# A retention layer with routed experts: when the first expert's weights are loaded, who stores the layer's rows, and the order of a few matmuls

## The chip, the core and the metric

The kernel runs on one core of a Trainium2 chip. The metric is the device time of one execution in microseconds: 736.68 us, the median of three runs (736.45 to 738.42). The profile is one further execution, of 732.8 us from the first instruction to the last; all times "at" a point below are counted from that start. The engines are named as in the profile: PE (matmuls) and PEld (its weight loads), DVE (VectorE), ACT (ScalarE), POOL (GpSimd) and SP (the engine that only issues transfers).

## What is computed

A retention layer (attention with a decay and no softmax) is followed by a layer of eight experts. A token takes either the expert with the highest logit or, when its "local gate" is 0.5 or more, the expert of the token before it; so the choice runs along the sequence.

```python
# attention: q, k, v are (8, 8, 576, 64), float32
scores = scale * np.matmul(q, k.transpose(0, 1, 3, 2))
Dmat = np.where(rel >= 0, gamma[:, None, None] ** rel[None, :, :], 0.0)
x = np.matmul(scores * Dmat[None], v)          # then (B, H, S, D) -> (B, S, H*D) = (8, 576, 512)
# experts: w1 (8, 512, 1024), w2 (8, 1024, 512)
logits = np.einsum('bsd,de->bse', x, w_gate)
local_gate = 1.0 / (1.0 + np.exp(-np.einsum('bsd,de->bse', x, w_local).squeeze(-1)))
for b in range(B):
    for s in range(S):
        fresh_e = int(np.argmax(logits[b, s]))
        e = fresh_e if s == 0 or local_gate[b, s] < 0.5 else prev_e
        prev_e = e
        out[b, s] = softmax(logits[b, s])[e] * (np.maximum(x[b, s] @ w1[e], 0.0) @ w2[e])
```

There are 4608 tokens of 512 features.

## The kernel before

**Attention (lines 145 to 252).** The tokens are cut into 36 chunks of 128. Nine chunks (two sequences of 576) make a period; `m` is a chunk's place in it. For a chunk, `scores` has SP load 1 MB (`ld`: q and k by feature, k and v by token) into one of seven buffers, DVE multiplies q by the decay (`qT`, line 165), POOL multiplies v by it (`vs`, line 169, four buffers), PE forms the scores of the chunk with itself (`sps`, line 176), and DVE masks them (`sT`, line 180). `outputs` multiplies them by `vs` (`ops`, line 201), adds the product of the queries with the state of all earlier chunks of the sequence (line 210), and ACT copies the result to `xT` (line 213). `state` adds the chunk's keys and values to that state (`kv`, line 227; ACT copies it, line 230). `rows` forms the gate products of the chunk (`gps`, line 238: four matmuls, one per 128 features, into four separate strips of 32 partitions; ACT copies them to `parts`, line 241), and turns the rows for storing (line 247, DVE). After every second chunk ACT issues four stores (line 250) of 128 KB each to `xd` in memory, 256 pieces of 512 bytes each. `logits` sums the four strips with one more matmul (`lps`, line 260).

The order on PE is written by hand: at step `i` come the scores of chunk `i + 1`, the outputs of chunk `i`, the state of chunk `i + 1`, the rows of chunk `i - 1`, the logits of chunk `i - 2`, then one step of each running routing. On the other engines a scheduler sets the order by what is ready. All transfers issued by SP and ACT share eight completion slots in turn, so an issue waits until the transfer eight before it has landed, whoever issued that one.

**Routing (lines 267 to 374 and 492 to 627).** Logits are collected in groups of chunks (`GROUPS`, 8, 8, 6, 7 and 7 of them) and ACT copies a group to `lt` (line 265). Then `route` finds each token's expert and its place among that expert's tokens, in a chain of some 45 small operations that goes from DVE to PE and back three times. When the last group is done, DVE and POOL build `values` (line 549), PE sums them (`places`, line 108) into the list of slots, and DVE derives which block takes which tokens (`desc`).

**Experts (lines 633 to 811).** Tokens are worked on in blocks of one expert, up to 768 tokens each. Two blocks' weights (`w1s`, `w2s`) are in fast memory at a time. POOL gathers a block's rows from `xd` (line 640) and loads the next weights (line 674). In `block`, PE first finishes group 0 of the block before (`first_group`), then runs the first layer (line 745; eight passes `m`, each of four matmuls for every piece of at most 512 tokens; ACT applies the ReLU into `hT`, line 747), then the second layer for a narrow remainder (line 710) and for groups 1 and up of 128 tokens each (line 683; ACT scales the result into `ys`, line 687). POOL scatters `ys` to the output (line 662) in order: group 0 of the block before, groups 1 to 5, two narrow pieces, all behind the whole block (lines 797 to 799).

Two things fill the time of the last routing. An **early block** (`block(-1, TSOON)`, line 766) runs 256 tokens of expert 0 that were routed from the first three groups. Its weights, those of expert 0, are what lines 158 to 163 load: 16 pieces of 256 KB, w1 and w2 in turn, behind the loads of chunks 4, 6, ... 34. And in block 0 the rows are turned by PE (`turn`, line 727) between the matmuls of the early block's last group, instead of by DVE.

Of the kernel before, what the change touches and what calls it, by code (L numbers as in the profile page):

```python
# [12 lines left out]
F32 = mybir.dt.float32  # L13
# [19 lines left out]
HALF = S - P * MID  # L33
assert HALF == P // 2 and NTOK % (2 * S) == 0

GROUPS = (8, 8, 6, 7, 7)
Q = max(GROUPS)
assert sum(GROUPS) == NCH

SOON, TSOON = 3, 2 * P  # L40
FULL = 512
# [21 lines left out]
def kernel(  # L63
# [55 lines left out]
    with ExitStack() as part:  # L119
# [25 lines left out]
        def scores(i):  # L145
            m = i % PER
            g = chunks[i]
            ld = raw.tile([P, 4, D], F32, name="ld")
            if i == MID:
                nc.sync.dma_start(out=decq[:, m].rearrange("p c t -> p (c t)"), in_=dq[:, 1])  # L150
            elif 0 < i < PER:
                for c in range(HP):
                    nc.scalar.activation(decq[:, m, c], decq[:, 0, c], Act.Copy, scale=later_q[:, m, c:c + 1])
            cut = 4 if i == 0 else 1
            for k in range(0, 4, 4 // cut):
                loaded = nc.sync.dma_start(out=ld[:, k:k + 4 // cut].rearrange("p t x -> p (t x)"),
                                           in_=qkv[i][:, k * D:(k + 4 // cut) * D])
            if 4 <= i < 4 + 4 * FK and i % 2 == 0:

                k, t = divmod(i // 2 - 2, 2)  # L160
                with tc.issue_after(loaded.ins):
                    nc.sync.dma_start(out=(w2s[0][:, k] if t else w1s[0][:, k].rearrange("p k f -> p (k f)")),
                                      in_=(w2 if t else w1)[0][:, k * D:(k + 1) * D])
# [5 lines left out]
            scaled = nc.gpsimd.tensor_tensor(  # L169
                vs.rearrange("p (h d) -> p h d", h=H), vn.rearrange("p (h d) -> p h d", h=H),  # L170
                deck[:, m, :].unsqueeze(2).to_broadcast([P, H, DH]), op=Alu.mult)
# [12 lines left out]

            with tc.issue_after(scaled.ins):
                for write in to_lanes[:2]:
                    write()
            del to_lanes[:2]

        def outputs(i):  # L190
            m = i % PER
            g = chunks[i]
            qT, vs, sT = g["qT"], g["vs"], g["sT"]


            ops = ps_o.tile([P, 2, HP, P], F32, name="ops")
            for c in range(HP):
                for u in range(2):
                    r = slice((u ^ c & 1) * DH, ((u ^ c & 1) + 1) * DH)
                    h = 2 * c + u  # L200
                    nc.tensor.matmul(ops[r, c & 1, c // 2, :], lhsT=vs[:, h * DH:(h + 1) * DH], rhs=sT[:, u, c, :],  # L201
                                     start=(c < 2), stop=(m == 0), skip_group_check=True)
# [9 lines left out]
            g["xT"] = xT = work.tile([P, HP, P], F32, name="xT", bufs=2)  # L212
            nc.scalar.copy(xT.rearrange("p (a b) t -> p b a t", b=2), ops[:, :, 0:HP // 2])  # L213

        def state(i):
# [14 lines left out]
                nc.scalar.copy(states[i % 2], kv)  # L230

        def rows(i):
            nonlocal x
            xT = chunks[i]["xT"]
# [5 lines left out]
            parts = work.tile([P, P], F32, name="parts")  # L240
            nc.scalar.copy(parts, gps)
            chunks[i]["parts"] = parts


            if i % 2 == 0:
                x = work.tile([P, 2, NSQ, DK, SQ], F32, name="x", bufs=2)
            nc.vector.transpose(x[:, i % 2], xT.rearrange("p c (t s) -> p t c s", s=SQ))  # L247
            if i % 2:
                for a in range(NSQ):
                    nc.scalar.dma_start(  # L250
                        out=xd[(i - 1) * P:(i + 1) * P, a * P:(a + 1) * P].rearrange("(t s) d -> s t d", s=SQ),
                        in_=x[a * SQ:(a + 1) * SQ].rearrange("p b t c r -> p (b t) (c r)"))

        def logits(i):

            nonlocal lt, lps
            i0 = max(k for k in starts if k <= i)
            if i == i0:
                lps = ps_g.tile([P, Q, GW], F32, name="lps")
            nc.tensor.matmul(lps[:, i - i0, :], lhsT=chunks[i]["parts"], rhs=add_parts, start=True, stop=True,  # L260
                             skip_group_check=True)
            if i in ends:
                n = i + 1 - i0
                lt = rt.tile([P, Q, GW], F32, name="lt")
                nc.scalar.copy(lt[:, 0:n], lps[:, 0:n])

# [181 lines left out]
        lt = lps = x = None  # L448

        add_parts = once.tile([P, GW], F32, name="add_parts")  # L450
        for c in range(DK):
            nc.gpsimd.tensor_copy(add_parts[c * SQ:(c + 1) * SQ], ident[c * SQ:(c + 1) * SQ, c * SQ:c * SQ + GW])
# [262 lines left out]
    def block(j, T):  # L715
# [4 lines left out]
        xT = xTs[j % 2]  # L720

        def turn(g, M):
            xps = next(hps_).rearrange("p (c t) -> p c t", c=DK)
# [33 lines left out]
        for g, M in groups[1:]:  # L757
            if M == P:
                group(j, g)

# [10 lines left out]
        weights(j + 1, False)  # L771
        load_tokens(j + 1)

    def store_rest(j):
        for g in range(1, GMAX):
            store(ys[:, g], rows_of[j % 2][:, g:g + 1])
        for M in NARROW:
            store(narrow_ys[M], narrow_rows[j % 2][M], P // M)
# [94 lines left out]
```

## Time and profile before

| stage of the profile | from, to (us) | what happens |
|---|---|---|
| attention | 0 to 170.8 | 36 chunks; `xT` of the first at 12.27, of the last at 168.71 |
| last routing, early block | 170.8 to 207 | PE begins the early block's first layer at 179.69, `places` at 194.75 |
| block 0 begins | 207 to 227.4 | group 0 of the early block and the turning of rows; first layer of block 0 at 227.44 |
| experts | 227.4 to 716.1 | PE busy throughout |
| end | 716.1 to 732.8 | last results copied and scattered; the program's end |

| engine | busy us | share of the span |
|---|---|---|
| PE | 688.8 | 94% |
| PEld | 455.2 | 62% |
| POOL | 232.9 | 32% |
| DVE | 182.1 | 25% |
| ACT | 145.0 | 20% |

The shares are averages over stages that differ: DVE, at 25% overall, is busy four fifths of the time in attention and nearly idle later. How to read the rows that follow: a group of instructions is written as line, engine, operation, what it writes and reads, shape and count, then busy time and the mean of one in ns, then how long the engine had been idle ahead of these instructions and what ended that idleness. A float32 matmul appears as two records, so 36 of them read x72. In the row of 40 slices, each digit is the busy share of a slice of 18.3 us in tenths, and PEclk is the clock granted to PE in tenths of full speed.

Transfers: 54.80 MB on SP's queue, 9.82 MB on ACT's and 50.36 MB on POOL's. The median load of a chunk lands 8.2 us after its issue, the median store of x rows after 5.3 us.

### The profile page before, as it was taken

How to read it: one execution, taken by the hardware profiler on the slowest of the kernel's cores; microseconds unless marked ns; L12 is line 12 of the kernel's file. 1: busy time of each engine (PE TensorE's matmuls, PEld its weight loads, DVE VectorE, ACT ScalarE, POOL GpSimd, SP SyncE). 2: the span in 40 equal slices, each digit the busy share in tenths (PEclk: the TensorE clock that was granted, in tenths of full speed). 3: DMA queues.
4: the chain of work that ended last, by engine and by line, in shares of the span. 5: the costliest groups of instructions: out<-in, count | busy, mean ns of one | idle time of the engine just before them, and what ended most of it. 6: DMA issues, size and time to landing. Idle time of an engine off the chain costs nothing. (4 is left out here: it accounts for less than half of the span.)

```text
span 732.8 us, 12623 instructions
## 1 busy us (share of the span) xinstructions
PE 688.8 (94%) x4960; PEld 455.2 (62%) x4960; DVE 182.1 (25%) x488; ACT 145.0 (20%) x375; POOL 232.9 (32%) x337
## 2 busy tenths in 40 slices
PE   5997999997989999999999999999999999999990
PEld 4876877785734547646754764675487467548640
DVE  5757769887900100200020010002001000200200
ACT  6221222223111112111211110221021112112100
POOL 5232525525270036008102700720270081035013
PEclk9998999997998999999999999999999999999996
DMA  8999999832085018405711740571175067014311
GB/s 336 335 345 356 382 348 339 302 96 51 2 254 116 1 47 303 94 3 206 229 24 62 298 107 3 178 242 33 57 284 128 7 229 199 4 62 140 74 36 49
DMA packets 72013, 116.55 MB, mean 159 GB/s; under 512 B 9160, under 2 KB 52300, under 8 KB 67408
## 3 DMA queue, kind: packets, MB, share of 16 engines
q1 hardware_dynamic: 34688, 54.80, 23.9%
q0 software_dynamic: 17184, 50.36, 18.8%
q10 hardware_dynamic: 20016, 9.82, 4.8%
q8 instruction: 66, 1.08, 0.7%
q14 instruction: 59, 0.48, 0.2%
HBM read 90.82 MB, written 24.12 MB: 157 GB/s over the span
## 5 line engine op out<-in xcount | busy, mean ns | idle before, releaser
L745 PE MATMUL hps<-xT,w1s 128*128 128x304 f32 (+4 forms) x1024 | 258.4, 414 | 0.7 <-ACT xT L729 0.7
L745 PEld LDWEIGHTS hps<-xT,w1s 128*128 128x128 f32 x1024 | 195.6, 191 | 65.0 <-issue 14.0
L683 PE MATMUL yps<-w2s,hT 128*128 128x512 f32 x528 | 232.5, 599 | 1.1 <-issue 1.1
L683 PEld LDWEIGHTS yps<-w2s,hT 128*128 128x128 f32 x528 | 100.0, 191 | 125.2 <-issue 124.9
L662 POOL DMA_INDIRECT out_dram<-ys,rows x49 | 48.8, 996 | 342.1 <-ACT ys L687 329.8
L747 ACT ACTIVATE hT<-hps 128x304 f32<-128x304 f32 (+4 forms) x128 | 53.1, 418 | 202.7 <-PE hps L745 193.7
L655 DVE STREAM_TRANSPOSE xT<-squares 128x512 f32<-128x512 f32 x48 | 29.4, 677 | 198.9 <-PE yps L710 150.7
L644 DVE CAST both<-slot 128x6 f32<-128x6 int32 x9 | 1.6, 172 | 259.0 <-POOL slot L638 259.0
L169 POOL TENSOR_TENSOR vs<-ld,decs 128x512 f32<-128x512 f32 x36 | 39.0, 1086 | 81.2 <-PE ops L201 42.1
L176 PE MATMUL sps<-qT,ld 64*128 64x128 f32 x576 | 49.1, 303 | 14.0 <-DMA ld<-in_qkv_dram 6.8
L640 POOL DMA_INDIRECT xg<-xd,slot x54 | 55.1, 1020 | 19.8 <-issue 13.0
L176 PEld LDWEIGHTS sps<-qT,ld 64*128 64x128 f32 x576 | 40.6, 202 | 17.4 <-DVE sT L180 8.6
L687 ACT ACTIVATE ys<-yps,slot 128x512 f32<-128x512 f32 x31 | 21.3, 688 | 147.3 <-PE yps L683 146.7
L180 DVE TENSOR_TENSOR sT<-sps,mask 128x512 f32<-128x512 f32 x72 | 45.8, 676 | 11.0 <-PE sps L176 10.3
L201 PE MATMUL ops<-sT,vs 128*64 128x128 f32 x576 | 42.4, 291 | 1.8 <-ACT xT L213 0.9
L213 ACT COPY xT<-ops 128x512 f32<-128x512 f32 x36 | 21.1, 587 | 111.4 <-PE ops L210 74.5
L201 PEld LDWEIGHTS ops<-sT,vs 128*64 128x64 f32 x576 | 33.1, 143 | 6.8 <-POOL vs L169 1.2
L165 DVE TENSOR_TENSOR qT<-ld,decq 128x512 f32<-128x512 f32 x36 | 31.4, 876 | 6.9 <-DMA ld<-in_qkv_dram 3.5
L247 DVE STREAM_TRANSPOSE x<-xT 128x512 f32<-128x512 f32 x36 | 25.3, 703 | 22.8 <-DMA xd<-x 18.3
L710 PE MATMUL yps<-w2s,hT 128*32 128x128 f32 (+1 forms) x544 | 30.1, 306 | 0.0
L710 PEld LDWEIGHTS yps<-w2s,hT 128*32 128x32 f32 (+1 forms) x544 | 21.2, 118 | 5.2
L227 PE MATMUL kv<-vs,ld 128*64 128x64 f32 (+1 forms) x512 | 22.5, 232 | 0.6 <-POOL one_of_blk L418 0.6
(194 smaller groups left out, 360.3 us busy)
## 6 DMA issues: line engine op xcount, KB each, us to landing
ld<-in_qkv_dram SPq DMA_DIRECT2D x35, 1024.0 KB, 8.2
w1s<-in_w_dram POOLq DMA_DIRECT2D x32, 512.0 KB
w2s<-in_w_dram POOLq DMA_DIRECT2D x32, 512.0 KB
squares<-xg SPq DMA_DIRECT2D x128, 96.0 KB, 2.3
xd<-x ACTq DMA_DIRECT2D x72, 128.0 KB, 5.3
w1s<-in_w_dram SPq DMA_DIRECT2D x8, 256.0 KB, 7.2
w2s<-in_w_dram SPq DMA_DIRECT2D x8, 256.0 KB, 6.7
ld<-in_qkv_dram SPq DMA_DIRECT2D x4, 256.0 KB, 5.8
```

What stands on the lines that cost most here:

```text
L165: nc.vector.tensor_tensor(qT, ld[:, 0].rearrange("p (c s) -> p c s", c=HP), decq[:, m], op=Alu.mult)
L169: scaled = nc.gpsimd.tensor_tensor(vs.rearrange("p (h d) -> p h d", h=H), vn.rearrange("p (h d) -> p h d", h=H), deck[:, m, :].unsqueeze(2 ...
L176: nc.tensor.matmul(sps[u][:, c, :], lhsT=kT[r, c, :], rhs=qT[r, c, :], start=True, stop=True, skip_group_check=True)
L180: nc.vector.tensor_tensor(sT[:, u], sps[u], (mask2 if m == MID else mask).unsqueeze(1).to_broadcast([P, HP, P]), op=Alu.mult)
L201: nc.tensor.matmul(ops[r, c & 1, c // 2, :], lhsT=vs[:, h * DH:(h + 1) * DH], rhs=sT[:, u, c, :], start=(c < 2), stop=(m == 0), skip_group ...
L640: nc.gpsimd.indirect_dma_start(out=xgs[j % 2][:, g, :], out_offset=None, in_=xd, in_offset=bass.IndirectOffsetOnAxis(ap=slot[:, g, 0:1], a ...
L655: nc.vector.transpose(xTs[j % 2][:, :, g * P:(g + 1) * P].rearrange("p c (t s) -> p t c s", s=SQ), squares[:, g].rearrange("p t (c r) -> p ...
L662: nc.gpsimd.indirect_dma_start(out=next(views).rearrange("t (q d) -> (t q) d", q=n), out_offset=bass.IndirectOffsetOnAxis(ap=rows, axis=0) ...
L683: nc.tensor.matmul(yps, lhsT=hT[:, m, g * P:(g + 1) * P], rhs=w[:, m, :], start=(m == 0), stop=(m == FK - 1))
L710: nc.tensor.matmul(yps[q * M:(q + 1) * M, 0:D // n], lhsT=hT[:, m, first:first + M], rhs=w[:, m, q * D // n:(q + 1) * D // n], start=(m == ...
L745: nc.tensor.matmul(hps[:, 0:T // n], lhsT=w[:, m, c, :], rhs=xT[:, c, cols], start=(c == 0), stop=(c == DK - 1))
L747: nc.scalar.activation(hT[:, m, cols], hps[:, 0:T // n], Act.Relu)
```

## The change

It has five parts.

1. The weights of the first expert no longer come between chunks 4 and 34. The eight pieces of w1 come behind the loads of the last eight chunks, and w2 comes in four pieces of 512 KB behind the last load. This leaves the early loads of q, k and v to themselves.
2. Gates of two chunks at once: `rows` runs on every second step for two chunks. Their products are summed over two of the four feature strips in place, so that both chunks fit into one tile of 128 partitions, and one copy and one logits matmul serve two chunks. The groups become 8, 8, 6, 8 and 6, all even.
3. In `outputs` the product with the past state stands ahead of the product with `sT`, so that PE has work that doesn't need the newest mask.
4. POOL issues the stores of x rows, so that ACT's queue, and the completion slots of the loads, are free of them. `xT` gets three buffers, `parts` two.
5. In the last block that is always run (`j == NSURE - 2`) the second layer of group 1 is taken out of the block and put behind a second branch. The stores of the narrow pieces and of groups 2 to 5 are issued ahead of it. In all blocks the narrow pieces are now stored first.

```diff
-GROUPS = (8, 8, 6, 7, 7)
+GROUPS = (8, 8, 6, 8, 6)
...
-            if 4 <= i < 4 + 4 * FK and i % 2 == 0:
-
-                k, t = divmod(i // 2 - 2, 2)
+            k = i - NCH + FK
+            if k >= 0:
                 with tc.issue_after(loaded.ins):
-                    nc.sync.dma_start(out=(w2s[0][:, k] if t else w1s[0][:, k].rearrange("p k f -> p (k f)")),
-                                      in_=(w2 if t else w1)[0][:, k * D:(k + 1) * D])
+                    nc.sync.dma_start(out=w1s[0][:, k].rearrange("p k f -> p (k f)"),
+                                      in_=w1[0][:, k * D:(k + 1) * D])
+            if i == NCH - 1:
+                for k in range(0, FK, 2):
+                    with tc.issue_after(loaded.ins):
+                        nc.sync.dma_start(out=w2s[0][:, k:k + 2].rearrange("p k f -> p (k f)"),
+                                          in_=w2[0][:, k * D:(k + 2) * D])
...
-            for c in range(HP):
-                for u in range(2):
-                    ...
-                    nc.tensor.matmul(ops[r, c & 1, c // 2, :], lhsT=vs[:, h * DH:(h + 1) * DH], rhs=sT[:, u, c, :],
-                                     start=(c < 2), stop=(m == 0), skip_group_check=True)
             if m > 0:
                 ...
                         nc.tensor.matmul(ops[r, c & 1, c // 2, 0:n], lhsT=states[(i + 1) % 2][k, c, :],
-                                         rhs=qT[k, c, 0:n], start=False, stop=True, skip_group_check=True)
+                                         rhs=qT[k, c, 0:n], start=(c < 2), stop=False, skip_group_check=True)
+            for c in range(HP):
+                for u in range(2):
+                    ...
+                    nc.tensor.matmul(ops[r, c & 1, c // 2, :], lhsT=vs[:, h * DH:(h + 1) * DH], rhs=sT[:, u, c, :],
+                                     start=(m == 0 and c < 2), stop=True, skip_group_check=True)
...
             for c in range(DK):
-                nc.tensor.matmul(gps[c * SQ:(c + 1) * SQ, :], lhsT=gates[:, c, :], rhs=xT[:, c, :],
-                                 start=True, stop=True, skip_group_check=True)
+                for b in range(2):
+                    r = slice((2 * b + c % 2) * SQ, (2 * b + c % 2 + 1) * SQ)
+                    nc.tensor.matmul(gps[r, :], lhsT=gates[:, c, :], rhs=xTs[b][:, c, :],
+                                     start=(c < 2), stop=(c >= 2), skip_group_check=True)
...
-            if i % 2:
-                for a in range(NSQ):
-                    nc.scalar.dma_start(
+            for a in range(NSQ):
+                nc.gpsimd.dma_start(
...
-            nc.tensor.matmul(lps[:, i - i0, :], lhsT=chunks[i]["parts"], rhs=add_parts, start=True, stop=True,
-                             skip_group_check=True)
+            nc.tensor.matmul(lps[:, i - i0:i - i0 + 2, :].rearrange("p c e -> p (c e)"), lhsT=chunks[i]["parts"],
+                             rhs=add_parts, start=True, stop=True, skip_group_check=True)
...
-                if 0 <= i - 1 < NCH:
-                    rows(i - 1)
+                if i % 2 == 0 and 0 <= i - 2:
+                    rows(i - 2)
                 if 0 <= i - 2:
-                    logits(i - 2)
+                    if i % 2:
+                        logits(i - 3)
...
+        apart = j == NSURE - 2
         for k in tc.Switch({ET.PE: kind, ET.Activation: kind}, len(SIZES) + 1):
             ...
             elif SIZES[k] and j < NBLK:
-                block(j, SIZES[k])
+                block(j, SIZES[k], 0 if apart else None)
         store(ys[:, 0], rows_of[j % 2][:, 0:1])
-        if j != NSURE - 1:
+        if apart:
+            store_rest(j, range(2, GMAX))
+            for k in tc.Switch({ET.PE: kind, ET.Activation: kind}, len(SIZES) + 1):
+                if k < len(SIZES) and SIZES[k]:
+                    block(j, SIZES[k], 1)
+            store_rest(j, (1,), ())
+        elif j != NSURE - 1:
             store_rest(j)
```

In the changed program's order, PE runs 7 of the 32 first-layer matmuls of the early block ahead of `places` and 25 behind it; in the program before these are 25 and 7. ACT's copies of the early block's turned rows stand, in the changed order, behind its twelve lane operations of the last group (lines 362 and 363 of the kernel before).

More of the change, by code (lines that the diff above doesn't have):

```diff
@@ L34 @@
 assert HALF == P // 2 and NTOK % (2 * S) == 0
-GROUPS = (8, 8, 6, 7, 7)
+GROUPS = (8, 8, 6, 8, 6)
 Q = max(GROUPS)
-assert sum(GROUPS) == NCH
+assert sum(GROUPS) == NCH and not any(n % 2 for n in GROUPS)
 SOON, TSOON = 3, 2 * P
@@ L196, in outputs @@
             ops = ps_o.tile([P, 2, HP, P], F32, name="ops")
-            for c in range(HP):
-                for u in range(2):
-                    r = slice((u ^ c & 1) * DH, ((u ^ c & 1) + 1) * DH)
-                    h = 2 * c + u
-                    nc.tensor.matmul(ops[r, c & 1, c // 2, :], lhsT=vs[:, h * DH:(h + 1) * DH], rhs=sT[:, u, c, :],
-                                     start=(c < 2), stop=(m == 0), skip_group_check=True)
             if m > 0:
@@ L210, in outputs @@
                         nc.tensor.matmul(ops[r, c & 1, c // 2, 0:n], lhsT=states[(i + 1) % 2][k, c, :],
-                                         rhs=qT[k, c, 0:n], start=False, stop=True, skip_group_check=True)
-            g["xT"] = xT = work.tile([P, HP, P], F32, name="xT", bufs=2)
+                                         rhs=qT[k, c, 0:n], start=(c < 2), stop=False, skip_group_check=True)
+            for c in range(HP):
+                for u in range(2):
+                    r = slice((u ^ c & 1) * DH, ((u ^ c & 1) + 1) * DH)
+                    h = 2 * c + u
+                    nc.tensor.matmul(ops[r, c & 1, c // 2, :], lhsT=vs[:, h * DH:(h + 1) * DH], rhs=sT[:, u, c, :],
+                                     start=(m == 0 and c < 2), stop=True, skip_group_check=True)
+            g["xT"] = xT = work.tile([P, HP, P], F32, name="xT", bufs=3)
             nc.scalar.copy(xT.rearrange("p (a b) t -> p b a t", b=2), ops[:, :, 0:HP // 2])
@@ L232, in rows @@
         def rows(i):
-            nonlocal x
-            xT = chunks[i]["xT"]
+            xTs = [chunks[i + b]["xT"] for b in range(2)]
             gps = ps_g.tile([P, P], F32, name="gps")
             for c in range(DK):
-                nc.tensor.matmul(gps[c * SQ:(c + 1) * SQ, :], lhsT=gates[:, c, :], rhs=xT[:, c, :],
-                                 start=True, stop=True, skip_group_check=True)
-            parts = work.tile([P, P], F32, name="parts")
+                for b in range(2):
+                    r = slice((2 * b + c % 2) * SQ, (2 * b + c % 2 + 1) * SQ)
+                    nc.tensor.matmul(gps[r, :], lhsT=gates[:, c, :], rhs=xTs[b][:, c, :],
+                                     start=(c < 2), stop=(c >= 2), skip_group_check=True)
+            parts = work.tile([P, P], F32, name="parts", bufs=2)
             nc.scalar.copy(parts, gps)
             chunks[i]["parts"] = parts
-            if i % 2 == 0:
-                x = work.tile([P, 2, NSQ, DK, SQ], F32, name="x", bufs=2)
-            nc.vector.transpose(x[:, i % 2], xT.rearrange("p c (t s) -> p t c s", s=SQ))
-            if i % 2:
-                for a in range(NSQ):
-                    nc.scalar.dma_start(
-                        out=xd[(i - 1) * P:(i + 1) * P, a * P:(a + 1) * P].rearrange("(t s) d -> s t d", s=SQ),
-                        in_=x[a * SQ:(a + 1) * SQ].rearrange("p b t c r -> p (b t) (c r)"))
+            x = work.tile([P, 2, NSQ, DK, SQ], F32, name="x", bufs=2)
+            for b in range(2):
+                nc.vector.transpose(x[:, b], xTs[b].rearrange("p c (t s) -> p t c s", s=SQ))
+            for a in range(NSQ):
+                nc.gpsimd.dma_start(
+                    out=xd[i * P:(i + 2) * P, a * P:(a + 1) * P].rearrange("(t s) d -> s t d", s=SQ),
+                    in_=x[a * SQ:(a + 1) * SQ].rearrange("p b t c r -> p (b t) (c r)"))
         def logits(i):
@@ L259, in logits @@
                 lps = ps_g.tile([P, Q, GW], F32, name="lps")
-            nc.tensor.matmul(lps[:, i - i0, :], lhsT=chunks[i]["parts"], rhs=add_parts, start=True, stop=True,
-                             skip_group_check=True)
-            if i in ends:
-                n = i + 1 - i0
+            nc.tensor.matmul(lps[:, i - i0:i - i0 + 2, :].rearrange("p c e -> p (c e)"), lhsT=chunks[i]["parts"],
+                             rhs=add_parts, start=True, stop=True, skip_group_check=True)
+            if i + 1 in ends:
+                n = i + 2 - i0
                 lt = rt.tile([P, Q, GW], F32, name="lt")
@@ L447 @@
         last_e = low[:, 0:1]
-        lt = lps = x = None
-        add_parts = once.tile([P, GW], F32, name="add_parts")
+        lt = lps = None
+        add_parts = once.tile([P, 2 * GW], F32, name="add_parts")
+        nc.gpsimd.memset(add_parts, 0.0)
         for c in range(DK):
-            nc.gpsimd.tensor_copy(add_parts[c * SQ:(c + 1) * SQ], ident[c * SQ:(c + 1) * SQ, c * SQ:c * SQ + GW])
+            r = slice(c * SQ, (c + 1) * SQ)
+            nc.gpsimd.tensor_copy(add_parts[r, c // 2 * GW:(c // 2 + 1) * GW], ident[r, c * SQ:c * SQ + GW])
         for M, at in ((P // 2, 0), (P // 4, 0), (P // 4, P // 2)):
@@ L713, in narrow, with block @@
         nc.scalar.activation(narrow_ys[M], yps[:, 0:D // n], Act.Copy, scale=share)
-    def block(j, T):
+    def block(j, T, part=None):
         xg = xgs[j % 2]
@@ L720, in block @@
         xT = xTs[j % 2]
+        if part == 1:
+            if groups[1:] and groups[1][1] == P:
+                group(j, 1)
+            return
         def turn(g, M):
@@ L756, in block @@
                 first += M
-        for g, M in groups[1:]:
+        for g, M in groups[1 if part is None else 2:]:
             if M == P:
@@ L772, in load_next, with store_rest @@
         load_tokens(j + 1)
-    def store_rest(j):
-        for g in range(1, GMAX):
+    def store_rest(j, groups=range(1, GMAX), sizes=NARROW):
+        for M in sizes:
+            store(narrow_ys[M], narrow_rows[j % 2][M], P // M)
+        for g in groups:
             store(ys[:, g], rows_of[j % 2][:, g:g + 1])
-        for M in NARROW:
-            store(narrow_ys[M], narrow_rows[j % 2][M], P // M)
     def step(j):
```

## Prediction

> **What bounds the kernel now.** I read the slices of the span first, then a table of stretches, then the groups, the waits and two spots of the timeline.
>
> ```profile
> PE   5997999997989999999999999999999999999990
> PEclk9998999997998999999999999999999999999996
> DMA  8999999832085018405711740571175067014311
> ```
>
> From the 13th slice on (220 us) PE is full to the end, so the change can shorten nothing of the expert stage but its last microseconds. What the change can move is the front: attention up to about 171 us, routing up to 227 us, and the tail. A table of stretches cuts the front (engine order: PE, PEld, DVE, ACT, POOL busy us with instruction counts, then clock, DMA share, GB/s):
>
> ```profile
> 24.00:54.00 30.00, 29.94 (x552) 24.43 (x548) 20.95 (x29) 7.61 (x21) 8.80 (x8) 1.00 0.91 323
> 54.00:60.00 6.00, 1.16 (x8) 0.97 (x9) 2.93 (x5) 0.88 (x4) 1.04 (x1) 0.70 1.04 342
> 60.00:96.00 36.00, 36.00 (x644) 29.63 (x642) 29.52 (x73) 8.98 (x25) 15.44 (x24) 0.95 1.02 378
> 96.00:102.00 6.00, 4.49 (x77) 3.46 (x77) 1.97 (x7) 1.81 (x6) 1.35 (x2) 1.00 0.90 298
> 102.00:141.00 39.00, 36.47 (x617) 29.40 (x621) 31.91 (x90) 9.13 (x28) 16.81 (x31) 1.00 1.00 346
> ...
> 192.00:195.00 3.00, 1.71 (x18) 1.52 (x17) 2.86 (x8) 0.21 (x1) 0.00 (x0) 1.00 0.03 8
> 195.00:207.00 12.00, 12.00 (x53) 7.46 (x50) 7.16 (x51) 0.77 (x2) 4.79 (x7) 1.00 0.39 124
> 207.00:227.44 20.44, 15.69 (x146) 7.64 (x146) 0.24 (x2) 3.00 (x7) 11.19 (x13) 0.83 0.64 195
> ```
>
> In attention PE is the bound with holes: from 24 to 141 us it is idle 0.06 + 4.84 + 0 + 1.51 + 2.53 = 8.9 us, 9.5 us to 171. The largest hole (54 to 60) is followed by three microseconds at half clock, 1.5 us more. DMA is full all that time, so the holes are loads that came late. The waits of the DMA issuer (SP) say why:
>
> ```profile
> SPq L156 <- DMA xd<-x: 36.7, 8, 8.9
> SPq L162 <- DMA xd<-x: 34.5, 9, 10.9
> ```
>
> SP stood 71 us behind stores of x: before it may issue a load, it waits for the completion slot that an earlier store of x, issued by ACT, still holds.
>
> Groups that price the edits (busy us, mean ns, idle before):
>
> ```profile
> L260 PE MATMUL lps<-add_parts,parts 128*128 128x10 f32 x72 | 14.0, 268 | 0.1
> L169 POOL TENSOR_TENSOR vs<-ld,decs 128x512 f32<-128x512 f32 x36 | 39.0, 1086 | 81.2 <-PE ops L201 42.1
> L640 POOL DMA_INDIRECT xg<-xd,slot x54 | 55.1, 1020 | 19.8 <-issue 13.0
> L674 POOL DMA_DIRECT2D w2s<-in_w_dram x32 | 15.8, 530 | 0.4 <-issue 0.2 <-DMA w2s<-in_w_dram 0.2
> ```
>
> And three instructions of the timeline: the copy that starts the last routing, the last result, the last store.
>
> ```profile
> 172.04 0.22 ACT L265 COPY lt<-lps 128x70 f32<-128x70 f32 x1 [1.71 <-DMA xd<-x]
> ...
> 716.14 0.69 ACT L687 ACTIVATE ys<-yps,slot 128x512 f32<-128x512 f32 x1 [0.48 <-PE yps L683]
> ...
> 720.63 0.98 POOL L662 DMA_INDIRECT out_dram<-ys,rows  x1 [0.30 <-issue]
> ```
>
> **What the Trainium skill says.** "DMA: Bandwidth & Descriptors", section "Issuing engines are not separate DMA queues": whoever issues, the transfers share the same 16 engines. So moving the x stores to GpSimd buys no bandwidth; the gain can only lie in who waits for whom. The trace agrees (DMA share 0.9 to 1.0 with three issuers). The same page, "SWDGE vs HWDGE vs iDMA": descriptors of a DMA issued by GpSimd are built in software there, so each costs that engine time; the trace has 0.53 to 1.02 us for one, against medians of 0.43 us on ACT's queue and 0.33 us on SP's. "SBUF — State Buffer", section "SBUF: two separate sides": while VectorE runs certain copies GpSimd cannot write descriptors, with 620 ns growing to 3100 in its example. Here the two indirect loads in attention, beside a VectorE busy 80%, took 1.14 us against 1.02 later: I expect little of it. "TensorE: Matmul & The Clock Gate", "What's actually happening": idle PE falls to half clock after about 3.4 us; the hole at 54 us agrees (clock 0.50 from 57 to 63).
>
> **The change part by part.**
>
> *Weights of the first expert* (16 loads of 256 KB in chunks 4 to 34; after: eight with chunks 28 to 35, then four of 512 KB). Same bytes, 4.2 MB; at the 378 GB/s of the stretch from 60 to 96 us 11 us of DMA leave the stretch in which PE starves. The late ones run behind SP's loads, where DMA before was busy 0.40 on average (141 to 171 us). They are needed at about 180 us: free. In the last eight chunks a load comes to 1.31 + 0.26 MB per chunk, 4.2 us; seven buffered chunks cover that.
>
> *x stores to GpSimd.* SP's 71 us behind stores vanish, so loads run up to seven ahead. Together with the weights I let this take 7 of the 11 us (9.5 of holes and 1.5 of half clock); VectorE, busy 29.52 of 36 us, so 3.2 us of a chunk step that shrinks to 3.8, keeps the rest. GpSimd gets 72 issues. Their cost isn't in the trace: each has 256 pieces of 512 B, where the direct weight load has 128 pieces (0.56 back to back) and the gather 128 rows (1.02, with 0.3 between). Bounds 0.56 and 1.3; I take 0.85. Total 61 us on top of 34 vs of 1.08 (37), 15 for lanes, 8 of casts and gathers: 121 of the 136 us from 20 to 156. Not the bound, though near it. Behind a waiting store stands the next vs; it runs about two chunk steps (7.6 us) ahead of its matmul, and four stores are 3.4: hidden.
>
> *Gates of two chunks at once.* The gate matmuls stay 8 per pair; the logits matmuls halve. One costs PE a step of 0.32 us (46.30 less 45.98 between starts in the timeline): 18 x 0.32 = **5.8 us** off the bound engine. The copies of parts (18 x 0.27 us of ACT) lie beside it: nothing.
>
> *Past states first.* The same matmuls in another order; the wait for sT is already short (PE waits 15 us for sT in all, before the scores): nothing counted apart from the holes.
>
> *Routing.* ACT no longer issues four stores before the logits copy: the 1.71 us wait goes, of which a step for the paired logits takes 0.7: -1.0. The last group has 6 chunks, not 7: -0.3. Against it, the order on PE: before, 25 of the 32 first-layer matmuls of the early block stand ahead of the matmuls that place the tokens, and 7 behind; after, 7 ahead and 25 behind. Moved behind: 18 x 0.434 = 7.8 us (each m of 4 took 1.73). ACT's copy into xT now also stands behind 12 lane operations, so PE begins the block some 5 us later. PE's holes ahead (2.6 us at 192) grow and pay nothing. What comes back: from 207 to 227.4 PE took 20.4 us for 7.0 of matmuls and some 4.7 of turns; it waited for gathers and instructions. With the early block later, gathers have landed and the weight loads of block 1 are mostly through; I take 16 us, bounds 12 and 20. Net -1.3 + 7.8 - 4.4 = **+2.1 us** (bounds -2 and +6.5).
>
> *Tail.* Before, eight stores of 1.3 us wait for the whole of block 7 and begin at 710.24; the last comes 5.5 us after PE ends (721.61 less 716.14). After, seven begin one group (6.86 us) earlier, and the last two fit right behind their results: 716.14 + 0.69 + 0.1 + 1.0 = 717.9, -3.7 us. The extra branch may cost up to 1 us: **-3.0**.
>
> Sum: -7 - 5.8 + 2.1 - 3.0 = -13.7; 736.68 - 13.7 = **723.0 us**.
>
> **The rivals.**
> - *All holes close.* -11 and -5.8 in attention, turns in 13 us (-0.9 in routing), tail -3.7: -21.4, 715 us. For it: PE is the one full engine. Against: VectorE at 85%.
> - *The routing eats it.* Holes refilled by vs or sT waits (-2), -5.8, +6.5, -2.5: -3.8, 733 us. For it: the moved 7.8 us stand on PE's path for sure.
> - *Nothing left.* As that one, with a GpSimd just at its limit that holds PE for 4 us: 737 us.
> - *GpSimd becomes the bound*, slower. At 1.3 us a store 94 + 59 = 153 us from 20 on: attention ends at 173, +2; routing +5, tail -3: 741 us. Half a microsecond more a store, if VectorE locks it out: 777. Against: the two gathers at 1.14.
>
> **How the numbers follow.** Forecast 0.58; all holes 0.14; routing eats it 0.11; nothing left 0.04; GpSimd bound 0.13. Faster 0.83, same 0.04, slower 0.13. The range leaves out the last two: from 713 (under the second case) to 735 (above the third).
>
> **What would show it.** Logits matmuls x36 at the same mean. SP without waits on xd. No stretch of attention under 90% PE; the last copy of xT (168.71 before) at 155 to 157. A store on GpSimd at 0.6 to 1.0 us. PE's first block-0 stretch at 215 to 217 instead of 227.4. Last store within 2 us of PE's end. Wrong if a store is over 1.1 us with vs waited for by PE, or if the early block begins later than 20 us behind the last xT.

## Result, and the profile after

The changed kernel takes **725.59 us** (median of 4 runs, 723.37 to 725.80) against 737.24 us (4 runs, 736.45 to 738.42): a ratio of 0.9834, 95% interval 0.9809 to 0.9858. The forecast was 723.0, with 713 to 735 as its range. Where some executions of a program were slow as a whole (two of the twelve of `e1_stores_act`), they count neither in its median nor in its ratio. The profiled executions of the two kernels span 732.8 and 723.8 us. The total came out close to the forecast: 11.7 us less by the medians, 9.0 in this pair of profiles, against 13.7. The parts did not, so they are set side by side first (us, from the timelines of the two profiles):

| step | before | after | difference | predicted |
|---|---|---|---|---|
| start to last copy of `xT` | 168.71 | 151.71 | -17.0 | -12.8 |
| last `xT` to first layer of block 0 | 58.73 | 64.13 | +5.4 | +2.1 |
| block 0 to PE's end | 488.66 | 491.55 | +2.9 | } |
| PE's end to last store's issue | 4.53 | 1.00 | -3.5 | } -3.0 |
| last store's issue to the end | 12.16 | 15.44 | +3.3 | } |
| sum | 732.8 | 723.8 | -9.0 | -13.7 |

The slices of the changed kernel (18.1 us each):

```profile
PE   5999998963999999999999999999999999999980
PEclk9999999995999999999999999999999999999996
DMA  8999999530462038218402830760184075024220
```

Attention ends one slice earlier, in the 9th, and a new hole stands in the 9th and 10th, the 10th at half clock. The table of stretches shows it (engine order PE, PEld, DVE, ACT, POOL, then clock, DMA share, GB/s):

```profile
24.00:60.00 36.00, 34.70 (x669) 29.67 (x669) 28.80 (x55) 10.15 (x26) 25.17 (x31) 1.00 1.02 415
60.00:96.00 36.00, 34.22 (x641) 29.45 (x640) 32.92 (x76) 9.15 (x24) 27.22 (x42) 0.95 0.95 348
96.00:120.00 24.00, 22.11 (x418) 18.70 (x414) 21.38 (x54) 6.20 (x17) 18.56 (x31) 1.00 1.01 389
...
159.00:172.00 13.00, 5.27 (x14) 4.08 (x15) 12.32 (x36) 4.51 (x15) 12.36 (x14) 0.61 0.00 1
172.00:186.00 14.00, 6.96 (x43) 5.99 (x43) 9.01 (x32) 0.38 (x1) 7.38 (x7) 0.63 0.00 1
```

From 24 to 60 us the transfers ran at a share of 1.02 and moved 415 GB/s; before, the stretches of that table with a share of 1.00 or more moved 342 to 378. From 159 to 186 us PE worked 12.2 of 27 us at a clock of about 0.6. The groups that were priced, and what SP now waits for (total, times, longest):

```profile
L266 PE MATMUL lps<-add_parts,parts 128*128 128x20 f32 x36 | 7.3, 279 | 0.4 <-ACT parts L248 0.4
L256 POOL DMA_DIRECT2D xd<-x x72 | 42.6, 597 | 12.0 <-DVE x L254 5.8 <-DVE run L309 1.9 <-DVE fr L298 1.8
L174 POOL TENSOR_TENSOR vs<-ld,decs 128x512 f32<-128x512 f32 x36 | 40.9, 1143 | 16.9 <-DMA ld<-in_qkv_dram 8.4 <-PE ops L215 5.3 <-issue 2.8
...
SPq L156 <- PE kv L232: 88.8, 26, 7.1
```

A store costs GpSimd 0.60 us, not the 0.85 taken. SP no longer waits for stores of x; it waits for buffers that PE has still to release, so loads run as far ahead as the seven buffers allow. Last, PE's way through the routing, before and after, and the last result and the last store after:

```profile
179.69 12.53 PE L745 MATMUL hps<-xT,w1s 128*128 128x256 f32 x50 [0.69 <-ACT xT L729]
193.51 3.58 PE L108 MATMUL places<-w1s,lanes 128*128 128x220 bf16 x36 [1.29 <-DVE first L573]
```

```profile
165.80 5.27 PE L758 MATMUL hps<-xT,w1s 128*128 128x256 f32 x14 [7.45 <-ACT xT L742]
179.04 5.71 PE L108 MATMUL places<-w1s,lanes 128*128 128x220 bf16 x36 [7.97 <-DVE its_n L606]
...
707.43 0.69 ACT L696 ACTIVATE ys<-yps,slot 128x512 f32<-128x512 f32 x1 [1.38 <-PE yps L692]
708.39 0.98 POOL L671 DMA_INDIRECT out_dram<-ys,rows  x1 [5.26 <-ACT ys L696]
```

The brackets are PE's idle time ahead of the early block's first layer and of `places`: 15.4 us together, against 2.0 before. In the profile before, `places` begins at 193.51; the 194.75 of the table of stages was the edge of a window.

### The profile page after: what moved, and what is told of

Same layout as the page of the kernel before. It is cut to its first block, busy times and chain, and to the rows that moved or that the text cites. A ratio compares the mean times of both kernels' runs of the same rounds, so it can differ in the third digit from the quotient of the medians.

```text
span 723.8 us, 12549 instructions
## 1 busy us (share of the span) xinstructions
PE 672.0 (93%) x4924; PEld 447.9 (62%) x4924; DVE 185.9 (26%) x488; ACT 141.6 (20%) x355; POOL 284.2 (39%) x411
## 4 chain that ended last, share of the span: by engine, by line
issue 56%; PE 16%; POOL 12%; DMA 8%; DVE 5%; POOLq 2%; ACT 0%; SPq 0%; DVEq 0%; ACTq 0%
POOL xg L649 5%; PE sps L181 4%; PE ops L215 4%; POOL out_dram L671 3%; DMA out_dram<-ys,rows 3%; DMA w2s<-in_w_dram 3%; PE ops L209 2%; PE kv L232 2%; PE gps L245 1%; DMA xd<-x 1%; POOL w1s L683 1%; PE places L108 1%; DVE sT L185 1%; DMA ld<-in_qkv_dram 1%; POOLq L683 1%
## 5 line engine op out<-in xcount | busy, mean ns | idle before, releaser
L758 PEld LDWEIGHTS hps<-xT,w1s 128*128 128x128 f32 x1024 | 195.8, 191 | 71.3 <-issue 13.7
L649 POOL DMA_INDIRECT xg<-xd,slot x54 | 54.8, 1015 | 21.1 <-issue 12.8
L181 PE MATMUL sps<-qT,ld 64*128 64x128 f32 x576 | 46.9, 295 | 11.2 <-DVE past L324 6.2
L181 PEld LDWEIGHTS sps<-qT,ld 64*128 64x128 f32 x576 | 38.8, 196 | 16.6 <-DVE sT L185 7.1
L174 POOL TENSOR_TENSOR vs<-ld,decs 128x512 f32<-128x512 f32 x36 | 40.9, 1143 | 16.9 <-DMA ld<-in_qkv_dram 8.4
L256 POOL DMA_DIRECT2D xd<-x x72 | 42.6, 597 | 12.0 <-DVE x L254 5.8
```

Source lines behind the costliest of these rows:

```text
L174: scaled = nc.gpsimd.tensor_tensor(vs.rearrange("p (h d) -> p h d", h=H), vn.rearrange("p (h d) -> p h d", h=H), deck[:, m, :].unsqueeze(2 ...
L256: nc.gpsimd.dma_start(out=xd[i * P:(i + 2) * P, a * P:(a + 1) * P].rearrange("(t s) d -> s t d", s=SQ), in_=x[a * SQ:(a + 1) * SQ].rearran ...
L649: nc.gpsimd.indirect_dma_start(out=xgs[j % 2][:, g, :], out_offset=None, in_=xd, in_offset=bass.IndirectOffsetOnAxis(ap=slot[:, g, 0:1], a ...
L758: nc.tensor.matmul(hps[:, 0:T // n], lhsT=w[:, m, c, :], rhs=xT[:, c, cols], start=(c == 0), stop=(c == DK - 1))
```

## The experiments

"Last xT" below is the start of the last copy of `xT`. In two profiles of the changed kernel itself it came at 151.71 and 148.37, so a difference of 3 us in one profile says little.

### Who stores x

`e1_stores_act`, the changed kernel with

```diff
-                nc.gpsimd.dma_start(
+                nc.scalar.dma_start(
```

> The changed kernel with one edit undone: ACT issues the x stores again. Theory (stores held the loads, so GpSimd's issues are worth most of the attention's gain): SP waits for completion slots of stores again (over 30 us), the last copy of xT moves from 151.7 to 156-162, median 727 to 732. Rival (weights and gates alone made the gain): last xT within 1 us of 151.7. On the end of the program: if its final drain on GpSimd, 8.9 us in the changed kernel and 6.0 before, grows with the number of GpSimd's transfers, it is back at 6.0 here; if it has another cause, it stays at 8.9.

```profile
SPq L156 <- DMA xd<-x: 38.5, 9, 7.9
SPq L156 <- DMA ld<-in_qkv_dram: 17.4, 5, 6.9
```

Measured: last xT at **168.43**, median 736.68 us (ten runs), ratio to before 0.9979 (0.9945 to 1.0013). One edit undone takes the whole gain, although weights, gates and order stay changed. SP waits behind slots again, 71 us up to the last xT (the two longest groups are shown). The theory's direction holds, but the effect is stronger than the 4 to 10 us expected of it, and its reason had to be tested. The drain at the end is back at 5.96 us.

`e12_act_long_pieces`: ACT issues, but in long pieces, which leaves the rows of x in other places than the gathers read.

```diff
-                nc.gpsimd.dma_start(
-                    out=xd[i * P:(i + 2) * P, a * P:(a + 1) * P].rearrange("(t s) d -> s t d", s=SQ),
-                    in_=x[a * SQ:(a + 1) * SQ].rearrange("p b t c r -> p (b t) (c r)"))
+                nc.scalar.dma_start(
+                    out=xd[i * P + a * 2 * SQ:i * P + (a + 1) * 2 * SQ].rearrange("(s t) d -> s (t d)", t=2),
+                    in_=x[a * SQ:(a + 1) * SQ].rearrange("p b t c r -> p (b t c r)"))
```

> As e1_stores_act (ACT issues the x stores, which hold completion slots as before), but each store of 128 KB goes out in 32 pieces of 4 KB instead of 256 of 512 bytes. The rows of x land in other places than the gathers expect, so the expert stage works on other rows in the same numbers. Theory (the 512-byte pieces of ACT's stores took the time of the transfers): last xT at 151 to 156 although ACT issues. Rival (it is ACT's queue or the slots, whatever the pieces): last xT at 163 to 169, as in e1 (168.4). The final drain: 6.0 us, since GpSimd issues no store of x.

```profile
SPq L156 <- DMA ld<-in_qkv_dram: 25.9, 7, 7.0
SPq L156 <- DMA xd<-x: 19.7, 8, 5.7
```

Measured: last xT at **147.00**, median 715.07 us, ratio 0.9700 (0.9637 to 0.9763). Same issuer and same slots as in e1, same bytes, 21 us apart: it is the size of the pieces. The transfers from 24 to 126 us (for each queue its packets, MB and share of 16 engines; q1 is SP's queue, q10 ACT's, q0 GpSimd's), first before, then the changed kernel, then e1, then e12:

```profile
DMA packets 17669, 35.42 MB, mean 347 GB/s; under 512 B 1316, under 2 KB 12902, under 8 KB 14477
q1 hardware_dynamic: 5347, 29.22, 76.8%
q10 hardware_dynamic: 12303, 5.93, 20.1%
```

```profile
DMA packets 7838, 39.25 MB, mean 385 GB/s; under 512 B 1426, under 2 KB 1426, under 8 KB 4191
q1 hardware_dynamic: 5329, 32.17, 80.8%
q0 software_dynamic: 2488, 6.79, 17.4%
```

```profile
DMA packets 16228, 32.59 MB, mean 320 GB/s; under 512 B 1161, under 2 KB 12611, under 8 KB 13101
q1 hardware_dynamic: 4053, 26.47, 71.5%
q10 hardware_dynamic: 12157, 5.87, 20.4%
```

```profile
DMA packets 7774, 39.00 MB, mean 382 GB/s; under 512 B 1439, under 2 KB 1439, under 8 KB 4138
q1 hardware_dynamic: 5155, 31.59, 81.0%
q10 hardware_dynamic: 2598, 7.12, 17.7%
```

Over the whole span, by the queue totals of each page less what the same queue carries without them, ACT's 72 stores are 19,584 packets (272 each: the 256 pieces and 16 more); GpSimd's stores of the same 512-byte pieces are 3,456 (48 each: 128 KB in 4 KB packets are 32, and 16 more), exactly as many as ACT's in 4 KB pieces. In the window of 102 us, a stored megabyte takes 20.1% of 102 us / 5.93 = 3.46 us of all 16 engines before and 17.4% of 102 us / 6.79 = 2.61 us after; a loaded one takes 2.68 and 2.56 us. For 9.44 MB of x and 42 MB of loads and weights the difference is 8.0 + 5.0 = 13 us of full transfers. By this estimate packets account for 13 of the 17 us; the rest lies within what gates and the spread between executions leave. The same sum from e1 to e12 (3.54 to 2.54 us for a stored megabyte, 2.76 to 2.62 for a loaded one) gives 9.5 + 5.9 = 15 of the 21 us. In e1 the transfers also stood still: its queues fill 93% of the window, against nearly 100% in e12, which is 7 us. What held them back there was not told apart.

`e10_slots_held` tests the other reason: GpSimd stores, and each store has a companion of 128 bytes from ACT that holds a slot.

```diff
+                nc.scalar.dma_start(out=held[i // 2, a:a + 1], in_=x[a * SQ:a * SQ + 1, 0, 0, 0])
```

> The changed kernel, with GpSimd's x stores kept, and beside each of them one store of 128 bytes from the same rows issued by ACT into a scratch area. It takes a completion slot and moves next to nothing. Theory (what held the loads before were the slots that stores held, not their bytes or pieces): SP waits for these stores (over 20 us), last xT at 160 to 169 as with ACT's stores (168.4), median 733 to 738. Rival (512-byte pieces from ACT's queue took the transfers' throughput): no wait of SP to speak of, last xT within 2 us of 151.7.

```profile
SPq L157 <- PE kv L233: 46.3, 13, 4.9
...
SPq L157 <- DMA ld<-in_qkv_dram: 31.5, 11, 3.9
SPq L157 <- DMA held<-x: 12.9, 5, 4.7
```

Measured: SP stands 44 us behind slots (13 of them behind the companions), yet last xT comes at 153.11, median 726.57 us. A companion holds its slot for less time than a real store would, so this alone would not exclude slots. But in e12 SP waits 22 us for stores of x and 32 us for loads ahead in the slots, and attention is as fast as in any run. So waiting for slots is not what cost the 17 us. A slot that a slow store holds for longer may still have a part in the 7 us in which e1's transfers stood still.

### Weights, gates, issues

`e2_weights_early` restores the loads behind chunks 4 to 34.

```diff
-            k = i - NCH + FK
-            if k >= 0:
...
+            if 4 <= i < 4 + 4 * FK and i % 2 == 0:
+                k, t = divmod(i // 2 - 2, 2)
```

> The changed kernel with the first expert's weights loaded among chunks 4 to 34 as before. Theory (4.2 MB at some 400 GB/s are 10 us of a full DMA, so they starve PE): last xT at 155 to 160, median 729 to 733, with waits of PE's scores for late loads. Rival (with GpSimd's stores the loads run seven chunks ahead and hide the weights anyway): last xT within 1 us of 151.7, median 725 to 726.5.

Measured: last xT at 151.82 against 151.71, median 726.43 us. The rival is right: beside GpSimd's stores, moving the weights is worth nothing that can be told. What it would be worth beside ACT's stores was not run.

`e5_gates_single` restores one tile, one copy and one logits matmul a chunk.

```diff
-                if i % 2 == 0 and 0 <= i - 2:
-                    rows(i - 2)
+                if 0 <= i - 1 < NCH:
+                    rows(i - 1)
...
-                    if i % 2:
-                        logits(i - 3)
+                    logits(i - 2)
```

> The changed kernel with the gates of each chunk by itself again (four strips, one copy, one logits matmul a chunk; groups stay 8, 8, 6, 8, 6). Theory (PE is the full engine of attention, so 18 logits matmuls of 0.32 us are on its path): last xT 5.8 us later, at 157.5, median 731. Rival (in attention PE now waits for DVE and loads often enough to hide them): last xT within 2 us of 151.7, median 725 to 727.

Measured: last xT at 152.80, but median 731.51 us (725.70 to 736.42, 10 runs), so it was run once more beside a control.

> The changed kernel itself, as a control beside the three others on one chip: 723 to 727, as before.

> The kernel with gates of single chunks once more, beside the control. Its profiled execution ended like the changed kernel's (724.1 against 723.8), while its timed runs spread from 725.7 to 736.4. Theory A (the pairing of gates is worth 5 us in a typical run, as the median 731.5 says, and the profiled run was the luckiest): median 4 to 7 us over the control on the same chip. Theory B (the spread came from the chip): within 1.5 us of the control.

Measured on one chip: control 727.77 us (722.31 to 730.88), single gates 730.50 (728.44 to 733.51); ratios to before 0.9868 (0.9823 to 0.9913) and 0.9882 (0.9839 to 0.9924). The second profile has its last xT at 158.37. Medians put the pairing at +2.7 us, which fits neither theory, the intervals overlap, and single profiles say +1.1 and +10. What it is worth stays open.

`e4_issues_x2` cuts each store in two.

```diff
-            for a in range(NSQ):
-                nc.gpsimd.dma_start(
-                    out=xd[i * P:(i + 2) * P, a * P:(a + 1) * P].rearrange("(t s) d -> s t d", s=SQ),
+            for a in range(NSQ):
+                for b in range(2):
+                    nc.gpsimd.dma_start(
+                        out=xd[(i + b) * P:(i + b + 1) * P, a * P:(a + 1) * P].rearrange("(t s) d -> s t d", s=SQ),
```

> The changed kernel with each x store cut in two: 144 stores of 64 KB and 128 pieces instead of 72 of 128 KB. If the final drain goes by the number of GpSimd's transfers it grows by another 2.9 us, from 8.9 to 11.8; if by bytes or pieces it stays at 8.9. If a store costs GpSimd the same 0.6 us whatever its pieces, GpSimd gets 43 us more in attention, is the bound there, and the last xT comes at 158 to 165 (median 734 to 742); if the cost goes by pieces (0.3 us), last xT stays within 1.5 us of 151.7.

```profile
L257 POOL DMA_DIRECT2D xd<-x x137 | 75.8, 560 | 9.1 <-DVE x L254 5.0 <-DMA xd<-x 2.3 <-issue 0.6
```

Measured (the line covers the first 160 us, 137 of the 144 stores): half a store costs 0.56 us, nearly as much as a whole one (0.60): GpSimd pays by the issue. Last xT comes at 159.61, GpSimd is busy 140.7 us up to there, and the median is 734.51 us, ratio 0.9967 (0.9948 to 0.9985). The forecast's rival of a GpSimd at its limit exists, 37 us of issues further on (79.6 us for all 144 against 42.6).

### The end

`e3_tail_whole`:

```diff
-        apart = j == NSURE - 2
+        apart = False
```

> The changed kernel without the second branch: the last sure block runs whole, its stores behind it. By the traces the branch holds PE for 0.8 + 1.6 = 2.4 us, and brings the last store from 5.5 to 2 us behind PE's end (3.5): theory says PE ends 2.4 us earlier, the last store starts 1.1 us later, median +1.1 us (726.7). Rival (the split was worth the 3.0 us forecast): median +3 (728.6). Second rival (it was worth nothing): within 0.5 us of 725.6.

Measured in its profile: from block 0 to PE's end 488.66 us, to the hundredth as before the change, against 491.55 with the branch; the last store starts 4.55 us behind PE's end instead of 1.00; from block 0 to the program's end 508.81 against 507.99. In this pair of profiles the split is worth **0.8 us**, near the first theory's 1.1. But nine profiles have the branch, GpSimd's stores and the changed kernel's experts, and over them PE's longer stop at the branch is 1.15 to 2.33 us and block 0 to the end 507.77 to 508.84 us. So the split is worth between nothing and 1 us, and the second rival (nothing) is not excluded. The median, 728.95 us (724.08 to 731.71), is too spread to add to this.

The other loss at the end is the drain of GpSimd (count, then shortest, median and longest duration in ns), before, after, and in e12:

```profile
L869 POOLq DRAIN  x3: 46/103/5957, 725.6 to 732.5; - x3
```

```profile
L891 POOLq DRAIN  x3: 46/103/8891, 714.1 to 723.5; - x3
```

```profile
L891 POOLq DRAIN  x3: 46/103/5957, 707.0 to 713.5; - x3
```

It takes 2.9 us more wherever GpSimd stores x, and 5.96 us in all three kernels where ACT does. It does not go by the number of stores: 144 instead of 72 (e4) take 9.06 us instead of 8.89. The bytes and pieces of e4 are those of the changed kernel, so by which of these it goes was not told apart.

### The routing

`e7_front_first` runs the early block's first layer ahead of `places`, and ACT's copies ahead of its lane operations.

```diff
+    block(-1, TSOON, "front")
+    with tc.issue_after(turned[0].ins):
+        late_lanes[0]()
...
-    block(-1, TSOON)
+    block(-1, TSOON, "rest")
```

> The changed kernel with another order after the last chunk: ACT copies the early block's turned rows ahead of its twelve lane operations, and PE runs all 32 first-layer matmuls of the early block ahead of the matmuls that place the tokens (7 in the changed kernel). Theory (the holes of 7.5 us before the first of them and 8.0 us before places are the routing's loss): early block's first layer at 158 instead of 165.8, places still at 179 (GpSimd's values come at 179.0), block 0's first layer at 204 to 208 instead of 215.8, median 714 to 718. Rival (block 0 waits for its gathered rows, which start at 189.7 either way): block 0 at 211 or later, median 721 to 725.

```profile
162.61 15.51 PE L608 MATMUL hps<-xT,w1s 128*128 128x256 f32 x64 [2.99 <-ACT xT L592]
180.18 3.58 PE L110 MATMUL places<-w1s,lanes 128*128 128x220 bf16 x36 [2.06 <-POOL w1s L656]
...
199.53 0.54 PE L590 MATMUL hps<-ident,xg 128*32 128x128 f32 x3 [1.07 <-issue]
200.96 0.59 PE L590 MATMUL hps<-ident,xg 128*32 128x128 f32 x3 [0.89 <-issue]
202.41 0.64 PE L590 MATMUL hps<-ident,xg 128*32 128x128 f32 x4 [0.87 <-issue]
```

The holes ahead shrink from 15.4 to 5.1 us, and all 32 matmuls lie before `places`. But from last xT to block 0 it takes 60.6 us instead of 64.1: 3.5 us come back, not ten. Block 0 starts at 213.61, inside the rival's range. What was won is lost in the turns, where PE now stands a microsecond after every three or four records. The median is 721.86 us, ratio 0.9768 (0.9707 to 0.9829): the fastest of the study but for e12, and faster than both kernels by its median, though its interval overlaps that of the changed kernel.

`e7b_values_first` adds

```diff
+    with tc.issue_after(by_pool.ins):
         for t in (ys, *narrow_ys.values()):
             nc.gpsimd.memset(t, 0.0)
```

> As e7_front_first, and GpSimd makes its fifth of the values ahead of clearing ys (2.65 us) instead of behind it. Theory: places starts 2.6 us earlier, at 176, gathers and block 0 follow: another 2 to 3 us, median 711.5 to 715.5. Rival (DVE's own share or PE's order sets places): no change against e7_front_first within 1 us.

Measured against `e7_front_first`: from last logits copy to `places` 24.1 us instead of 25.1, from there to block 0 36.9 instead of 33.4; median 724.58 us. The theory's 2 to 3 us did not come. The gain ahead is again lost in the turns.

`c1_gathers_later` is `e7b_values_first` with block 1's gathers moved:

```diff
-        if j != NSURE - 1 and j + 1 < NBLK:
+        if j == 0:
+            weights(1, False)
+        elif j != NSURE - 1 and j + 1 < NBLK:
             load_next(j)
...
         store(ys[:, 0], rows_of[j % 2][:, 0:1])
+        if j == 0:
+            load_tokens(1)
```

> As e7b_values_first, and block 1's six gathers are issued behind block 0's first store instead of ahead of it. In the changed kernel, in e7 and before, PE stands still a microsecond at a time (released by nothing the trace shows) between the turns just while these gathers run. Theory (they starve PE of instructions): turns run through, block 0's first layer at 203 to 207 instead of 214.2, median 713 to 717. Rival (PE waits there for something else, block 0's rows or the branch): block 0 at 212 or later, median 721 to 725.

```profile
192.14 1.94 PE L590 MATMUL hps<-ident,xg 128*32 128x128 f32 x32
194.00 1.17 PE L542 MATMUL yps<-w2s,hT 128*128 128x512 f32 x2
195.10 1.08 PE L590 MATMUL hps<-ident,xg 128*32 128x128 f32 x32
...
202.30 22.51 PE L608 MATMUL hps<-xT,w1s 128*128 128x416 f32 x64
...
285.25 15.06 PE L608 MATMUL hps<-xT,w1s 128*128 128x288 f32 x52 [37.45 <-DVE xT L766]
```

With the gathers gone from this stretch the turns run through, and block 0 starts 27.7 us after `places` instead of 36.9. (In e7, with the same order and the gathers in place, it is 33.4.) The theory holds that far: the stops in the turns come from the neighbour's gathers. The transfers that rearrange the gathered rows moved with them, but in e7b they start at 206.93, behind the stops (198.9 to 205.4). How the gathers stop PE is not shown. The kernel is slower all the same, 754.58 us, ratio 1.0233 (1.0183 to 1.0282): the store that the gathers now stand behind waits until ACT has left block 0 (241.94), and PE waits 37.45 us for block 1's rows. A place between the two was not tried. Part 3 of the change was not run by itself either.

## Why the prediction was right, and where it was not

The total is inside the range because a gain taken too small, for a wrong reason, met losses also taken too small. That they nearly cancelled is luck, and so is block 0's start at 215.84, where 215 to 217 had been forecast.

- *x stores to GpSimd.* That stores held the loads, and that GpSimd's issues would free them, came true in the waits. But the step behind it, that a slot's wait was what cost time and that another issuer "buys no bandwidth", failed: e1 against e12 shows that the pieces, and with them the packets, cost most of it. The section of the Trainium skill on issuing engines is true as it stands (the transfers do share the 16 engines); the error was to conclude that the same bytes would take the same time of them. The Trainium skill's page "DMA: Bandwidth & Descriptors", section "SWDGE vs HWDGE vs iDMA", says that GpSimd's transfers go in packets of up to 4096 bytes by preference, which the 48 packets a store fit (32 of 4 KB and 16 small ones). Section "Why small descriptors are slow (HBM only)" says that joining pieces is worth it only up to 256 bytes; here pieces of 512 gained from it (3.46 to 2.61 us a megabyte), and the measurement decides.
- *Weights.* The 7 us were put down to them and the freed loads together; e2 gives the weights 0.1.
- *Gates.* The instruction is what was said (records of 279 ns against 268, and half as many). Whether all 5.8 us lie on the path is what e5 left open.
- *GpSimd as the bound.* Rightly rejected: a store cost 0.60 us, not the 0.85 taken; e4 shows how near the bound is.
- *No stretch under 90% PE.* Wrong: in the seventh slice (108.6 to 126.7 us) PE works 15.4 of 18.1 us, 85%, though each row of the table above that lies in attention is over 90%. PE's waits in attention are now for DVE's masks (4.2 us in all) and routing results (1.3).
- *Routing.* The faster logits copy came (3.33 to 2.14 us, -1.2 for -1.3). From the end of `places` to block 0 the sum was +3.4 and the trace has +0.75: the 7.8 us of 18 matmuls moved behind, and the turns gave nearly all of it back. The mis-sized term is the one set to nothing ("PE's holes ahead grow and pay nothing"; the hole named there is 1.29 us long, not 2.6): from the logits copy to the end of `places` it takes 30.90 us instead of 25.06. GpSimd's share of the values stands behind eight lane operations and the clearing of `ys` and ends at 178.99, 7.5 us after DVE's. Then `places` takes 5.71 us instead of 3.58: behind 7.97 us of idleness the clock granted from 179 to 183 us is 0.50.
- *The starving turns*, priced at 16 us instead of 20.4 because gathers would have landed: right in direction and too small, 13.3 us from ACT's copy of the early block's group 1 to block 0 (202.52 to 215.84; before 207.10 to 227.44). c1 agrees with the reason. The Trainium skill's "Runtime: NRT & Kernel Launch", section "Instruction fetch mechanics", says that a taken branch makes the engine wait for a fetch when its target is not among the instructions already loaded; block 0 lies behind a branch, and the stops carry no releaser. That it is the fetch which the gathers slow is a guess from this; no run here shows it.
- *Tail.* The last store came 1.0 us behind PE, as forecast (-3.5). The branch, allowed 1 us, cost 0.78 + 1.61 us of PE; the 2.9 us by which the drain grew were not in the sum at all. In the profiles the tail became 2.7 us longer, where 3.0 less had been forecast.

Of the rivals, "all holes close" had the size of attention's gain (16.8 us against 17.0), also by a reason that does not hold; "the routing eats it" named the losses of the routing.

## What to carry to other kernels

Where transfers are the full resource, count their packets beside their bytes: the same 9.4 MB in 512-byte packets, or in 4 KB ones, were 21 us apart in a stage of 168 (e1 and e12), with the same issuer, most of it by the time that the packets take. A theory about waits needs a run in which the wait is there and the suspected cost is not (e12), since a wait that vanishes together with a cost proves nothing. And the time of a stage that is made of small instructions behind a branch depends on what its neighbours transfer just then, so an order that fills a hole ahead of it may win little.

## What the runs showed of the hardware

GpSimd's stores of 512-byte pieces leave as 4 KB packets, 48 a store against ACT's 272. An issue costs GpSimd 0.56 to 0.60 us whether it has 128 or 256 pieces. Its drain at the program's end grows from 5.96 to 8.89 us with the stores of x, and hardly with their number (9.06 us for twice as many). Six row gathers beside a branched stretch of PE cost it 6 to 9 us (e7 and e7b against c1, one profile each).
